# P times V of a sliding-window attention kernel on two 64-row tiles

## The chip, the cores and the metric

The kernel runs on one core of a Trainium2 chip. The metric is device time in microseconds, the time of the whole program. The kernel before took 688.97 us in the median of 3 runs (688.08 to 691.63).

## What is computed

One layer mixes two branches over a sequence of 2048 positions of width 512. Branch A is attention with 32 heads of 16 dimensions, in which a query sees its own key and the 255 before it; branch B is a layer norm and a two-layer MLP with 1792 hidden units. A gate per position adds them.

```python
qkv = (x @ wqkv).reshape(B, S, 3, H, Dh).transpose(2, 0, 3, 1, 4)      # H = 32, Dh = 16, W = 256
scores = einsum("bhqd,bhkd->bhqk", q, k) * Dh ** -0.5
mask = (idx[:, None] - idx[None, :] >= 0) & (idx[:, None] - idx[None, :] < W)
p = softmax(where(mask, scores, -1e9), axis=-1)
o = einsum("bhqk,bhkd->bhqd", p, v)                                     # "P times V"
a = o.transpose(0, 2, 1, 3).reshape(B, S, D) @ wo
b = gelu(layernorm(x) @ w1 + b1) @ w2 + b2
out = g * a + (1 - g) * b                                               # g = sigmoid(sum(x * gate_w))
```

## The kernel before, in words

The program has three stages. The first computes q, k and v and the layer norm's statistics. The second, from about 150 to 487 us, does the attention and the MLP's first layer together; the change lies in it. The third computes the attention's output projection and the MLP's second layer. The program's order within an engine is the order in which the Python code issues it: a manual schedule is set, so nothing is moved afterwards.

The second stage is a string of steps written out by hand, `ORDER` (line 38). Each letter is one step that `run` (line 748) issues:

- **S** is `s_pair` (line 353): scores of 128 queries against up to 384 keys for two of the four heads of a pass, only to find the maximum of each query. TensorE writes a pair of PSUM banks (line 362), and VectorE reads it: `copy_predicated` (line 371) folds the mask's corner in, and `tensor_reduce` (line 372) takes the maximum. For the first two query blocks it is line 368 instead.
- **T** is `st_pair` (line 409): the same scores turned round, 128 keys by up to 384 queries, for two heads (line 418). ScalarE takes the exponential out of PSUM into a tile `pts[p, kb]` (line 420), and GpSimd cuts the window's two edges to zero (line 422). A tile `pts[p, kb]` holds four heads by 384 queries for the 128 keys of block `kb`.
- **P** is `pv` (line 429): for four heads and 256 queries (step `j` of 8) it multiplies the `pts` tiles of up to four key blocks by v. v has 17 columns a head, the last of ones, so that the sum of the weights comes out as well, and 32 are loaded. Two P in a row, where the first has an even `j`, become one of 512 queries (`both`).
- **f** is `fill` (line 719): one step of the MLP's first layer, two matmuls of 64 rows and 512 columns (line 651), 24 such steps to a unit. A unit ends with two copies by ScalarE (`copy`, line 136) and two stores.

P is written out on the array as follows. `a` is one bank; head `h` goes to partitions `32 * h` to `32 * h + 32` and so to its own column tile, `tile_position=(0, 32 * h)`, over all 128 rows. The inner products of one key block are cut out at whole blocks of 128 queries: for a step of 256 queries the pieces are 256, 128, 256 and 128 columns wide (768 for each head), and for 512 queries 256, 128, 384, 384, 256 and 128 (1536). The first step of a pass has the last two of four, or the last four of six. The result is copied by ScalarE into `s` (line 449 or 453, recorded at line 136), or, once the S steps have run out (`last`), by VectorE (line 451). Every 512 queries `s` is stored (line 458 through SyncE, one step later; line 460 through ScalarE's queue at the end).

S, T, P and a unit of f each take a pair of PSUM banks from a ring of four pairs, b0 to b3 (`two`, line 117; `choose`, line 114). `PICK` (line 51) says for each whether the oldest pair is taken or the next. A unit of f keeps its pair over 24 steps, so three are left to S, T and P in the meantime. A pair can be written again when the engine that empties it has done so: VectorE for S, ScalarE for T, P and f.

Of the kernel before, what the change touches and what calls it, by code (L numbers as in the profile page):

```python
# [17 lines left out]
ALU = mybir.AluOpType  # L18
# [14 lines left out]
VW = 17  # L33
# [28 lines left out]
def gated_mix_kernel(ctx, tc: tile.TileContext, xt, x2, wq0, wqk, wv, wo, xa, gw, w1, w2, b1, b2, out):  # L62
    nc = tc.nc
    dve, act, pool, pe, sp = nc.vector, nc.scalar, nc.gpsimd, nc.tensor, nc.sync
# [18 lines left out]
    def get(key, tag, bufs, shape, dt=F32):  # L83
        return left[key].tile(list(shape), dt, name=nm(tag), tag=tag, bufs=bufs)
# [18 lines left out]
    def ps(tag, shape=(128, 512)):  # L103
        key, bufs = banks[tag]
        return left[key].tile(list(shape), F32, name=nm("ps_" + tag), tag=tag, bufs=bufs)
# [3 lines left out]
    def pair(tag):  # L109
        if tag not in pairs:  # L110
            pairs[tag] = ps(tag, (128, 2, 512))
        return pairs[tag]

    def choose():
        return ring.pop(int(picks.pop(0)) if picks else 0)

    def two():
        if not ring:
            return ps("x", (128, 2, 512))
        ring.append(choose())  # L120
        return pair(ring[-1])
# [13 lines left out]
    def copy(dst, src):  # L135
        act.activation(dst, src, AF.Copy)  # L136
# [4 lines left out]
    def after(k, fn):  # L141
        todo.setdefault(step[0] + k, []).append(fn)
# [25 lines left out]
    vs = get("ring", "v", 1, (128, NB, VR))  # L168
# [184 lines left out]
    def s_pair(p, qb, pr):  # L353
        if qb == 0 and pr == 0:
            mxs[p] = small("mx", 2, (128, 2, 2, NB))
        assert qb * 128 < held_cols[p]
        n = min(qb + 1, 3) * 128
        t0 = qb * 128 + 128 - n
        o = two()
        for e in range(2):  # L360
            r, k = ((0, 62), (64, 112))[e]
            pe.matmul(o[:, e, :n], qs[pr][r:k, qb * 128:qb * 128 + 128], ks[pr][r:k, t0:t0 + n],  # L362
                      start=True, stop=True)
        m = mxs[p][:, pr, :, qb]
        if qb < 2:
            for e in range(2):
                sc = small("scr", 2, (128, 256), BF16)
                dve.tensor_tensor_reduce(out=sc[:, :n], in0=o[:, e, :n], in1=wide[:, 256 - n:], scale=1.0, scalar=NEG,
                                         op0=ALU.add, op1=ALU.max, accum_out=m[:, e:e + 1])
        else:  # L370
            dve.copy_predicated(o[:, :, :128], tri, o[:, :, 256:384])  # L371
            dve.tensor_reduce(m, o[:, :, :256], mybir.AxisListType.X, ALU.max)  # L372
        if pr and qb % 4 == 3:
            put_max(p, qb - 3)
# [32 lines left out]
    pts, acc = {}, {}  # L407

    def st_pair(p, kb, pr):
        w = min(NB - kb, 3) * 128  # L410
        assert ("m", p, (kb * 128 + w - 1) // 512) in done
        if pr == 0:
            pts[p, kb] = p_tile()
        pt = pts[p, kb][:, 2 * pr:2 * pr + 2]
        o = two()
        for e in range(2):
            r, k = ((0, 64), (64, 114))[e]
            pe.matmul(o[:, e, :w], ks[pr][r:k, kb * 128:kb * 128 + 128], qs[pr][r:k, kb * 128:kb * 128 + w],  # L418
                      start=True, stop=True)
        act.activation(pt[:, :, :w], o[:, :, :w], AF.Exp, scale=0.25)  # L420
        for a, sgn, b in ((0, 1, 0), (256, -1, -1))[:1 + (w == 384)]:
            pool.affine_select(out=pt[:, :, a:a + 128], in_=pt[:, :, a:a + 128], pattern=[[0, 2], [sgn, 128]],  # L422
                               base=b, channel_multiplier=-sgn, compare_op=ALU.is_ge, fill=0.0)

    def flush():
        while late:
            late.pop(0)()

    def pv(p, j, last, both):
        flush()  # L430
        a = two()[:, 0]
        if both:
            parts = ((-1, 0, 128, 256), (-2, 0, 256, 128), (0, 0, 0, 384), (1, 128, 0, 384), (2, 256, 0, 256),
                     (3, 384, 0, 128))[0 if j else 2:]
        else:
            parts = ((-1, 0, 128, 256), (-2, 0, 256, 128), (0, 0, 0, 256), (1, 128, 0, 128))[0 if j else 2:]
        for n, (d, at, fr, w) in enumerate(parts):
            kb = 2 * j + d
            for h in range(4):
                v = (4 * p + h) * VW  # L440
                pe.matmul(a[32 * h:32 * h + 32, at:at + w], vs[:, kb, v:v + 32], pts[p, kb][:, h, fr:fr + w],  # L441
                          start=n == 0, stop=n == len(parts) - 1, skip_group_check=True, tile_position=(0, 32 * h))
        if j % 2 == 0:
            sums.append(sums.pop(0))
            acc[p] = sums[-1]
        s = acc[p]
        o = j % 2 * 256
        if both:
            copy(s, a)
        elif last:  # L450
            dve.tensor_copy(s[:, o:o + 256], a[:, :256])
        else:
            copy(s[:, o:o + 256], a[:, :256])
        if j % 2 or both:
            j += both
            to = osc[p, :, (j - 1) * 256:(j + 1) * 256]
            if lt:
                after(1, lambda: sp.dma_start(to, s))
            else:
                act.dma_start(to, s)  # L460
# [258 lines left out]
    def fill():  # L719
        if cur[0] is None:  # L720
            assert {("w", jobs[0][0]), ("y", jobs[0][1], KT - 1)} <= done
            cur[0] = mlp1_unit(*jobs.pop(0))
        if next(cur[0], 0) == 0:
            cur[0] = None

    def block(p, kb):
        if kb % 2 == 0:
            if kb and p + 1 < 8:
                load_stacks(p + 1, kb * 128 - 256, 256)
            if not kb and p:  # L730
                load_stacks(p, S - 256, 256)
        tick()
        if p in (0, 2, 4) and kb % 2 == 0:
            double(p // 2 + 1, kb // 4, 1 - kb // 2 % 2)
        if p == 7 and kb == LAG:
            early_w2()
        if p == 7 and kb == 12:
            early.extend(load_h(0, f) for f in range(2))
        if p == 7 and kb == 13:
            early_wo(0, 2)  # L740
# [4 lines left out]
    ls = [(p, qb, pr) for p in range(8) for qb in range(NB) for pr in range(2)][2 * (NB - LAG):]  # L745
    lp = [(p, j) for p in range(8) for j in range(NB // 2)]

    def run(order):
        skip = False
        for a, b in zip(order, order[1:] + " "):  # L750
            if skip:
                skip = False
                continue
            spot[0] += 1
            for n in sorted(n for n in soons if n <= spot[0]):
                for fn in soons.pop(n):
                    fn()
            flush()
            if a == "T":
                p, kb, pr = lt.pop(0)  # L760
                if not pr:
                    block(p, kb)
                st_pair(p, kb, pr)
            elif a == "S":
                s_pair(*ls.pop(0))
            elif a == "P":
                p, j = lp.pop(0)
                skip = b == "P" and j % 2 == 0
                if skip:
                    lp.pop(0)  # L770
                pv(p, j, not ls, skip)
                spot[0] += skip
            else:
                fill()

    run(ORDER + 6 * "f")
    flush()
    for f, (gelu, _) in enumerate(early):
        gelu()
    held = {"b0", "b1", "b2", "b3"} - set(ring)  # L780
    for x in held:
        mate = x[0] + str(int(x[1]) ^ 1)
        ring.remove(mate)
        ring.insert(0, mate)
    run("P")
    ring.insert(0, ring.pop())
    used = {ring[0]} | held
# [184 lines left out]
```

## Time and profile before

| what | value |
|---|---|
| median of the runs | 688.97 us (688.08 to 691.63) |
| the profiled execution's own time | 689.64 us |
| its span, first to last instruction | 687.8 us |
| granted TensorE clock | 0.999 |
| TensorE, VectorE, ScalarE, GpSimd busy | 681.1, 476.4, 384.6, 265.9 us |
| second stage, P: matmul records, steps | 1856 records, 60 steps (4 of them of 512 queries) |
| second stage, P: evacuations | 54 by ScalarE, 6 by VectorE |

All durations in the text come from this one execution, whose own time is 0.67 us above the median. In a row of the groups or of the timeline stand the line, the engine, the operation, what it writes and reads, the shapes and the number of instructions; PE is TensorE's matmuls and PEld its weight loads, DVE is VectorE, ACT ScalarE and POOL GpSimd. A copy through `copy` stands at line 136 whatever it copies. The first number of a timeline row is its start in us from the span's start, the second the time that it covers, and a bracket gives the idle time of the engine before it and what ended that. A full-precision matmul of P stands in the records twice: the code issues 928 and the profile has 1856.

### The profile page before, as it was taken

To read this page: it belongs to the slowest core of one execution; us is meant where nothing else is said; L and a number is where in the kernel's file an instruction comes from. 1 tells how busy PE (TensorE), PEld (TensorE's weight loads), DVE (VectorE), ACT (ScalarE), POOL (GpSimd) and SP (SyncE) were. 2 spreads that over 40 slices of the span, in tenths; PEclk is the share of its full clock that TensorE was granted. 3 is DMA by queue.
4 is the path that set the end of the run, shared out by engine and by line. 5 is a ranking of instruction groups with operands and counts; after the bars stand their busy time and mean duration, and the time that the engine had idled before them with its cause. 6 is when DMAs were issued, how large, how long until landed. Compare 5 with 4: busy or idle time off the path is not lost.

```text
span 687.8 us, 15593 instructions
## 1 busy us (share of the span) xinstructions
PE 681.1 (99%) x5674; PEld 535.5 (78%) x5674; DVE 476.4 (69%) x970; ACT 384.6 (56%) x637; POOL 265.9 (39%) x622
## 2 busy tenths in 40 slices
PE   9999999999999999999999999999999999999997
PEld 6887777877768777877787777777787888888886
DVE  6737789968777787777686877855575545556454
ACT  6438453457677776877758777687633224123231
POOL 6800156426666664765656566568000000000000
PEclk9999999999999999999999999999999999999999
DMA  8998888786575767566676555527876450841801
GB/s 322 354 290 266 278 262 267 217 253 224 176 211 173 247 211 228 174 214 188 190 240 207 168 185 153 178 96 240 288 238 204 143 173 5 275 126 41 253 1 62
DMA packets 89620, 137.91 MB, mean 200 GB/s; under 512 B 13160, under 2 KB 36648, under 8 KB 89416
## 3 DMA queue, kind: packets, MB, share of 16 engines
q1 hardware_dynamic: 81384, 128.72, 59.1%
q10 hardware_dynamic: 8160, 8.19, 3.9%
q8 instruction: 45, 0.74, 0.4%
q14 instruction: 31, 0.25, 0.1%
HBM read 81.53 MB, written 54.30 MB: 197 GB/s over the span
## 4 chain that ended last, share of the span: by engine, by line
PE 96%; ACT 1%; DVE 1%; DMA 1%; issue 0%; POOL 0%; SPq 0%; DVEq 0%; ACTq 0%
PE ps_b L651 22%; PE ps_a L881 22%; PE ps_b L441 13%; PE ps_d L308 12%; PE ps_b L418 7%; PE ps_b L362 7%; PE ps_d L338 7%; PE ps_o L850 6%; PE ps_d L295 1%; PE ps_x L362 1%; DMA qk<-qk 1%; PE ps_x L279 1%; ACT x L420 0%; DVE us L895 0%; DVE us L889 0%; ACT pb L420 0%
## 5 line engine op out<-in xcount | busy, mean ns | idle before, releaser
L651 PE MATMUL ps_b<-x,w 64*128 64x512 f32 x1344 | 207.1, 393 | 0.0
L881 PE MATMUL ps_a<-x,t 128*128 128x512 f32 x648 | 150.2, 389 | 0.2 <-DVE t L711 0.2
L372 DVE TENSOR_REDUCE mx<-ps_b 128x2 f32<-128x512 f32 x208 | 144.1, 693 | 7.1
L881 PEld LDWEIGHTS ps_a<-x,t 128*128 128x128 f32 x648 | 121.5, 188 | 26.2 <-DVE t L711 0.6
L651 PEld LDWEIGHTS ps_b<-x,w 64*128 64x128 f32 x1344 | 127.4, 186 | 10.5 <-ACT x L136 0.3
L371 DVE COPY_PREDICATED ps_b<-tri,ps_b 128x256 f32<-128x256 uint8 x208 | 88.4, 425 | 52.7 <-PE ps_b L362 40.6
L422 POOL TENSOR_SCALAR_AFFINE_SELECT pa<-pa 128x256 f32<-128x256 f32 x192 | 74.2, 414 | 57.7 <-ACT pa L420 56.7
L420 ACT ACTIVATE pa<-ps_b 128x768 f32<-128x768 f32 x96 | 76.5, 813 | 24.7 <-PE ps_b L418 13.3
L418 PE MATMUL ps_b<-qk 50*128 50x384 f32 (+5 forms) x512 | 87.8, 339 | 0.1
L308 PE MATMUL ps_d<-x,w 128*128 128x512 f32 x360 | 84.7, 390 | 0.0
L362 PE MATMUL ps_b<-qk 62*128 62x384 f32 (+3 forms) x472 | 83.0, 345 | 1.0 <-DMA qk<-qk 0.8
L308 PEld LDWEIGHTS ps_d<-x,w 128*128 128x128 f32 x360 | 67.3, 188 | 14.5 <-issue 0.5
L420 ACT ACTIVATE pb<-ps_b 128x768 f32<-128x768 f32 (+2 forms) x96 | 66.2, 706 | 20.5 <-PE ps_b L418 9.7
L422 POOL TENSOR_SCALAR_AFFINE_SELECT pb<-pb 128x256 f32<-128x256 f32 x160 | 62.2, 415 | 37.4 <-ACT pb L420 36.9
L707 ACT ACTIVATE t<-t,b1s 128x512 f32<-128x512 f32 x56 | 38.6, 716 | 44.0 <-DMA t<-hp 43.6
L418 PEld LDWEIGHTS ps_b<-qk 50*128 50x128 f32 (+1 forms) x512 | 48.8, 184 | 16.0 <-issue 3.2
L422 POOL TENSOR_SCALAR_AFFINE_SELECT x<-x 128x256 f32<-128x256 f32 x128 | 49.3, 414 | 29.7 <-ACT x L420 29.3
L420 ACT ACTIVATE x<-ps_b 128x768 f32<-128x768 f32 x64 | 50.7, 813 | 14.0 <-PE ps_b L418 9.7
L362 PEld LDWEIGHTS ps_b<-qk 62*128 62x128 f32 (+1 forms) x472 | 45.1, 184 | 17.2 <-issue 3.9
L338 PE MATMUL ps_d<-wv,x 128*128 128x512 f32 x192 | 46.7, 394 | 0.0
L850 PE MATMUL ps_o<-w,t 128*128 128x512 f32 x192 | 46.1, 389 | 0.0
L441 PE MATMUL ps_b<-pa,v 128*32 128x128 f32 (+2 forms) x704 | 42.9, 345 | 0.3 <-ACT x L420 0.2
(96 smaller groups left out, 757.1 us busy)
## 6 DMA issues: line engine op xcount, KB each, us to landing
qk<-qk SPq DMA_DIRECT2D x112, 196.0 KB
t<-hp SPq DMA_DIRECT2D x56, 256.0 KB
hp<-t SPq DMA_DIRECT2D x54, 256.0 KB
qk<-t SPq DMA_DIRECT2D x48, 256.0 KB
osc<-x SPq DMA_DIRECT2D x31, 256.0 KB
t<-in_w SPq DMA_DIRECT2D x28, 256.0 KB
w<-w SPq DMA_DIRECT2D x28, 256.0 KB
qk<-t ACTq DMA_DIRECT2D x24, 256.0 KB
```

The lines of the kernel that those rows point to most:

```text
L308: pe.matmul(o, a[:, dt * 128:(dt + 1) * 128], b[:, dt * C:(dt + 1) * C], start=n == 0, stop=n == 11)
L338: pe.matmul(o, x[:, a:a + 128], wvs[dt][:, k], start=n == 0, stop=n == 11)
L362: pe.matmul(o[:, e, :n], qs[pr][r:k, qb * 128:qb * 128 + 128], ks[pr][r:k, t0:t0 + n], start=True, stop=True)
L371: dve.copy_predicated(o[:, :, :128], tri, o[:, :, 256:384])
L372: dve.tensor_reduce(m, o[:, :, :256], mybir.AxisListType.X, ALU.max)
L418: pe.matmul(o[:, e, :w], ks[pr][r:k, kb * 128:kb * 128 + 128], qs[pr][r:k, kb * 128:kb * 128 + w], start=True, stop=True)
L420: act.activation(pt[:, :, :w], o[:, :, :w], AF.Exp, scale=0.25)
L422: pool.affine_select(out=pt[:, :, a:a + 128], in_=pt[:, :, a:a + 128], pattern=[[0, 2], [sgn, 128]], base=b, channel_multiplier=-sgn, comp ...
L441: pe.matmul(a[32 * h:32 * h + 32, at:at + w], vs[:, kb, v:v + 32], pts[p, kb][:, h, fr:fr + w], start=n == 0, stop=n == len(parts) - 1, sk ...
L651: pe.matmul(o[:, e], w[kt // 4][r:r + 64, k, m:m + 128], y[r:r + 64, a:a + C], start=n == 0, stop=n == 23)
L850: pe.matmul(a, x[:, g], wos[g][:, k], start=n == 0, stop=n == 11)
L881: pe.matmul(accs[c][b], x[:, b * 128:(b + 1) * 128], w, start=f == 0 and n == 0, stop=f == FT - 1 and n == 2)
```

## The change

`pv` no longer multiplies all 128 keys of a block at once. It takes the upper and the lower 64 keys apart: rows 0 to 63 of the array for the one and rows 64 to 127 for the other (`tile_position=(64 * r, 32 * h)`), with the result of each in a bank of its own of the pair that `two` gives. Each half has its own span of queries: 64 keys reach 320 queries, not 384. The pieces of a half are sorted by width, widest first, and the two lists are issued side by side: four matmuls (one a head) of the upper half, four of the lower, then the next pieces. For 256 queries that makes pieces of 256, 192, 128 and 64 columns in each half. At the end ScalarE copies the first bank into `s`, and VectorE adds the second bank to it. The branch for `last` is gone, so the six steps whose result VectorE copied have ScalarE's copy and VectorE's sum too. `ORDER`, `PICK`, the ring and every other step are as they were.

```diff
-    def pv(p, j, last, both):
+    def pv(p, j, both):
         flush()
-        a = two()[:, 0]
-        if both:
-            parts = ((-1, 0, 128, 256), (-2, 0, 256, 128), (0, 0, 0, 384), (1, 128, 0, 384), (2, 256, 0, 256),
-                     (3, 384, 0, 128))[0 if j else 2:]
-        else:
-            parts = ((-1, 0, 128, 256), (-2, 0, 256, 128), (0, 0, 0, 256), (1, 128, 0, 128))[0 if j else 2:]
-        for n, (d, at, fr, w) in enumerate(parts):
-            kb = 2 * j + d
-            for h in range(4):
-                v = (4 * p + h) * VW
-                pe.matmul(a[32 * h:32 * h + 32, at:at + w], vs[:, kb, v:v + 32], pts[p, kb][:, h, fr:fr + w],
-                          start=n == 0, stop=n == len(parts) - 1, skip_group_check=True, tile_position=(0, 32 * h))
+        a = two()
+        q, w = 256 * j, 512 if both else 256
+        parts = []
+        for r in range(2):
+            seen = []
+            for kb in range(max(2 * j - 2, 0), 2 * j + w // 128):
+                k = kb * 128
+                fr, to = max(q, k + 64 * r * (kb > 0)), min(q + w, k + 64 * r + 320)
+                seen.append((fr - to, kb, fr - q, to - q, fr - k, to - k))
+            parts.append(sorted(seen))
+        for n, pieces in enumerate(zip(*parts)):
+            for r, (_, kb, *at) in enumerate(pieces):
+                rows = slice(64 * r, 64 * r + 64)
+                for h in range(4):
+                    v = (4 * p + h) * VW
+                    pe.matmul(a[32 * h:32 * h + 32, r, at[0]:at[1]], vs[rows, kb, v:v + 32], pts[p, kb][rows, h, at[2]:at[3]],
+                              start=n == 0, stop=n == len(parts[0]) - 1, skip_group_check=True, tile_position=(64 * r, 32 * h))
...
-        if both:
-            copy(s, a)
-        elif last:
-            dve.tensor_copy(s[:, o:o + 256], a[:, :256])
-        else:
-            copy(s[:, o:o + 256], a[:, :256])
+        copy(s[:, o:o + w], a[:, 0, :w])
+        dve.tensor_tensor(out=s[:, o:o + w], in0=a[:, 1, :w], in1=s[:, o:o + w], op=ALU.add)
```

More of the change, by code (lines that the diff above doesn't have):

```diff
@@ L770, in run @@
                     lp.pop(0)
-                pv(p, j, not ls, skip)
+                pv(p, j, skip)
                 spot[0] += skip
```

## The prediction, made before the changed kernel was run

> **What bounds the kernel now.** I read the page's totals and its chain first, then the waits of the second stage, then P's groups by shape, then the timeline around single P steps.
>
> ```profile
> PE 681.1 (99%) x5674; PEld 535.5 (78%) x5674; DVE 476.4 (69%) x970; ACT 384.6 (56%) x637; POOL 265.9 (39%) x622
> PE 96%; ACT 1%; DVE 1%; DMA 1%; issue 0%; POOL 0%; SPq 0%; DVEq 0%; ACTq 0%
> ```
>
> TensorE is busy all the time and carries 96% of the chain. So TensorE's columns are what the change can save, and TensorE's waiting is what it can cost. The waits of the second stage (150 to 490 us), matmuls first, weight loads below, say how much waiting there is:
>
> ```profile
> PE ps_b L362 <- DMA qk<-qk: 0.8, 1, 0.8
> PE ps_b L441 <- ACT x L420: 0.2, 1, 0.2
> PEld ps_b L441 <- ACT x L136: 5.6, 23, 0.3
> ```
>
> The matmuls waited 1.0 us in 340. The weight loads waited more, and the third row tells where: in 23 of the 60 P steps the load stood until ScalarE's copy of a P (line 136 into x) had ended, 0.24 us each. That is the copy of the P before: the next one takes the same PSUM pair. It shows only at the loads, because TensorE has just come out of other matmuls; but nothing is left over there. The timeline shows one such place whole:
>
> ```profile
> 165.01 0.16 PEld L441 LDWEIGHTS ps_b<-pa,v 128*32 128x32 f32 x8 [0.25 <-ACT x L136]
> 165.01 0.64 PE L441 MATMUL ps_b<-pa,v 128*32 128x256 f32 x8
> ...
> 165.69 0.62 PE L441 MATMUL ps_b<-pb,v 128*32 128x256 f32 x8
> ...
> 166.12 0.40 PE L441 MATMUL ps_b<-x,v 128*32 128x128 f32 x8
> 166.45 0.30 PEld L362 LDWEIGHTS ps_b<-qk 62*128 62x128 f32 x4 [0.20 <-ACT pb L420]
> 166.45 0.61 PE L362 MATMUL ps_b<-qk 62*128 62x384 f32 x4
> 166.59 0.39 ACT L136 ACTIVATE x<-ps_b 128x256 f32<-128x256 f32 x1 [0.30 <-PE ps_b L441]
> ...
> 166.90 0.34 PE L418 MATMUL ps_b<-qk 64*128 64x384 f32 x2
> 167.00 0.43 DVE L371 COPY_PREDICATED ps_b<-tri,ps_b 128x256 f32<-128x256 uint8 x1 [0.90 <-ACT x L136]
> 167.17 0.16 PEld L441 LDWEIGHTS ps_b<-x,v 128*32 128x32 f32 x8 [0.25 <-ACT x L136]
> ```
>
> A P runs from 165.01 to 166.45, 1.44 us. Two S and a T follow, 0.72 us. ScalarE copies P's result from 166.59 to 166.98. At 167.17, 0.19 us after the copy, the next P starts on the same pair. So the pair is wanted again 0.72 us after P's matmuls, and the copy takes 0.53 of these.
>
> **TensorE's columns.** P's matmul groups by shape:
>
> ```profile
> L441 PE MATMUL ps_b<-pa,v 128*32 128x256 f32 x320 | 25.3, 388 | 0.3 <-ACT x L420 0.2
> L441 PE MATMUL ps_b<-pb,v 128*32 128x256 f32 x320 | 24.8, 381 | 0.0
> L441 PE MATMUL ps_b<-x,v 128*32 128x256 f32 x256 | 20.1, 385 | 0.0
> L441 PE MATMUL ps_b<-pa,v 128*32 128x128 f32 x320 | 16.4, 273 | 0.0
> L441 PE MATMUL ps_b<-pb,v 128*32 128x128 f32 x320 | 16.1, 273 | 0.0
> L441 PE MATMUL ps_b<-x,v 128*32 128x128 f32 x256 | 13.1, 273 | 0.0
> L441 PE MATMUL ps_b<-pa,v 128*32 128x384 f32 x64 | 6.0, 490 | 0.0
> ```
>
> These are 896 records of 256 columns, 896 of 128 and 64 of 384. Four heads run side by side and every matmul is recorded twice, so divided by 8 they make 46,080 columns, each passed twice. The price is in the timeline: the eight records that start at 165.69 (four heads of 256 columns, twice) give way to the next at 166.12, so 512 columns take 0.43 us, 0.84 ns a column. P's streaming is 46,080 x 2 x 0.84 ns = 77.4 us. The mean durations in the rows are no price; records overlap.
>
> After the change the two halves lie on different rows and in different banks, and I let them run together: a step costs the wider piece of each pair. That is 640 columns for 51 of the steps (256, 192, 128 and 64 in place of 768), still 384 for the five first steps of 256 queries, 1088 in place of 1152 for three first steps of 512, and 1280 in place of 1536 for one. The sum is 39,104, that is 6,976 fewer, and 6,976 x 2 x 0.84 ns = **11.7 us saved**, 0.22 us on a usual P. That halves run together is shown by the MLP steps, which set two matmuls of 64 rows beside each other (the pairs of 64x512 below), and four column tiles beside each other by P itself; eight tiles at once no row shows.
>
> The narrowest piece, 64 columns, must cost its 0.054 us and not more. The nearest rows are a T of 128 columns and what follows it:
>
> ```profile
> 312.24 0.23 PE L418 MATMUL ps_b<-qk 64*128 64x128 f32 x2
> 312.30 0.45 PE L651 MATMUL ps_b<-x,w 64*128 64x512 f32 x2
> ```
>
> The next pair starts 0.06 us behind it and runs 0.06 longer than the 0.39 of its group: a load of 128 weights a row takes about 0.12 us of the array, so I estimate a quarter, 0.03, for 32, which fits under 0.054. From the other side, a piece of 128 columns now takes 0.11 us; if that were a floor, 52 pieces, twice each, would give back 52 x 2 x 0.054 = 5.6 us. I take nothing, and keep 5.6 for the range.
>
> The eight records that start at 165.69 show no sum of starts: four tiles take exactly the 0.84 ns a column that the streaming asks. [...]
>
> **The second bank.** Every P gets a VectorE sum out of PSUM, behind ScalarE's copy:
>
> ```profile
> L451 DVE COPY x<-ps_b 128x256 f32<-128x256 f32 x6 | 2.6, 426 | 12.1 <-PE ps_b L441 7.0 <-DMA hp<-t 5.1
> L889 DVE TENSOR_TENSOR us<-ps_a,b2s 128x512 f32<-128x512 f32 x4 | 2.5, 682 | 0.0
> L133 DVE TENSOR_TENSOR w<-wv,w 128x128 fp32r<-128x128 f32 x8 | 2.1, 289 | 0.6 <-ACT w L136 0.4
> ```
>
> A sum over 512 columns takes 0.68 us, one over 128 takes 0.29, so over 256 0.42; the copy of 256 takes 0.43. Work for VectorE: 56 x 0.42 + 4 x 0.68 less the six copies of 0.43 = 23.7 us, over a stage in which it has this load:
>
> ```profile
> 250.00:300.00 50.00, 50.00 (x646) 38.67 (x644) 38.23 (x86) 37.34 (x58) 31.05 (x83) 1.00 0.64 201
> ```
>
> 38.2 us of 50 (third pair), 76%; with 23.7 more in 340 it is 83%. VectorE does not become the bound by its sum. What counts is when the pair is free: the sum waits for the copy, so it comes 0.42 + 0.05 (a handover) later. In the place above: 167.45 in place of 166.98, measured against the same end of P. P's being shorter doesn't help, since the 0.72 us between P's end and the next use hold only S and T. The next P starts 0.05 after the release, and has 0.19 now, so it comes 0.33 us late, and TensorE stands, since matmuls start in order. The other kind of place has an S, a T or an MLP unit on the pair next, not a P:
>
> ```profile
> 309.34 0.44 PE L418 MATMUL ps_b<-qk 64*128 64x384 f32 x2
> 309.54 0.38 ACT L136 ACTIVATE x<-ps_b 128x256 f32<-128x256 f32 x1 [0.63 <-PE ps_b L441]
> 309.62 0.63 PE L651 MATMUL ps_b<-x,w 64*128 64x512 f32 x4
> 309.97 0.18 PEld L418 LDWEIGHTS ps_b<-qk 64*128 64x128 f32 x2 [0.16 <-ACT x L136]
> 310.09 0.34 PE L418 MATMUL ps_b<-qk 64*128 64x384 f32 x2
> ```
>
> The copy ends at 309.92, the load starts at 309.97 and the matmul at 310.09, when the MLP pairs before it are through: a delay of 0.47 costs 0.45 here. Other places have more room. I take 0.33 us for each of the 54 steps that ScalarE empties now: **17.8 us**; bounds are none (the room is always found) and 54 x 0.47 = 25. The six last steps lose 0.39 (the copy ahead of the sum) where VectorE has few other tasks, about 1 us in all.
>
> Behind the sum, on VectorE, stand the S steps that TensorE issues right after P: at 167.00 above a `copy_predicated` starts that would wait until about 167.45. Their pairs come free as much later, but are wanted only after the user that already came 0.33 late; the rest is about 0.1 us a P where there is no room, at a third of the steps 2 us; bounds 0 and 5. The stores of `s` leave 0.5 us later through SyncE's queue, and the last one through ScalarE's; who reads them does so in the next stage, so nothing.
>
> **Sum.** -11.7 + 17.8 + 1 + 2 = +9 us, on the execution's 689.64, and as much on the median of 688.97: **698 us**.
>
> [...]
>
> **Rivals.**
>
> *The sum is hidden (faster).* If the next user of P's pair could start 0.47 us later without TensorE noticing, the 11.7 would remain, less some 2: 680 us. It decides at the room behind the copy: 0.05 to 0.2 us in the two places above, so it needs over twice that. For it: not every place is alike, and each wait lets ScalarE and VectorE catch up. Against it: 23 loads ended on this very copy.
>
> *The halves do not run together.* If the second half can only start when the first half's second pass does, each step gets a piece's length behind at every change of width, and 256+256+256+192+192+128+128+64+64 = 1536 passed columns are what 2 x 768 were. Nothing is saved, and the stalls stay: 709 us. If they ran one after the other it would be 77,312 columns, 52 us more than now, near 760. For it: eight tiles are not in the trace. Against: each of the two kinds of tiling is.
>
> *The way in and out gets cheaper.* Between 64-row and 128-row tiles there is a gap: the loads of 165.01 and 166.45 stood idle 0.25 and 0.20 us, of which about 0.1 at each end is no streaming. With 64 rows throughout, it may go. The gap behind P is part of the 0.72 us that cover the copy, so only the one ahead counts, 0.1 x 53 = 5 us: 693, no change. [...]
>
> **How the numbers follow.** The smallest change that a measurement of this kernel can tell is about 0.5%, 3.4 us: 685.5 to 692.4 is "same". The forecast (stalls outweigh columns) has 0.60, and alone reaches from 692 to 706. The hidden sum has 0.17, some of it ending just within "same". Halves apart have 0.11, all slower. The cheaper switch has 0.12, half of it within "same". Faster 0.16, same 0.14, slower 0.70. The range that holds it 8 times in 10 cuts off half the hidden cases and the serial ones: 684 to 712.
>
> **What would show it.** In the changed profile: P's records twice as many, 3712, a usual P 1.2 us long; in the waits of the weight loads VectorE's sum in the place of line 136, with matmuls now waiting 15 to 20 us on it in all; VectorE near 500 us busy. If P takes 1.4 us the halves do not overlap; if P takes 1.2 us and the matmuls hardly wait, the forecast is wrong by its stalls and the time is near 680.

## The result, and the profile after

The changed kernel takes **712.02 us** in the median of 4 runs (710.84 to 712.67) against 689.26 for the kernel before beside it (4 runs, 688.08 to 691.63): 1.0322 times as long, 95% interval 1.0302 to 1.0342. It is slower, as forecast, but by 22.8 us and not by 9, and lies 0.02 us beyond the range's upper end of 712. The profiled execution took 712.67 us at a granted clock of 0.999. The page's totals, its queue of instruction packets and its chain after the change:

```profile
PE 683.9 (96%) x7530; PEld 547.1 (77%) x7530; DVE 492.9 (69%) x1024; ACT 386.5 (54%) x643; POOL 268.7 (38%) x622
...
q8 instruction: 59, 0.97, 0.6%
...
PE 66%; DMA 10%; DVE 9%; ACT 7%; issue 3%; SPq 3%; POOL 2%; ACTq 0%; DVEq 0%
```

TensorE is busy 96% of the span where it was 99%, and other engines have come into the chain. The changed P has 7530 - 5674 = 1856 records more, hence 3712, as forecast. The second line belongs to the argument further down, where q8's packets are set against TensorE's instructions; before it read

```profile
q8 instruction: 45, 0.74, 0.4%
```

The waits of the second stage (150 to 515 us; the columns are us in total, times, longest) now say where TensorE stands:

```profile
PEld ps_b L446 <- issue: 16.6, 28, 1.5
PEld ps_b L418 <- DVE x L454: 8.6, 18, 0.7
PE ps_b L446 <- DVE x L454: 7.7, 19, 0.6
PEld ps_b L362 <- DVE x L454: 6.1, 10, 1.5
...
PE ps_b L362 <- DVE x L454: 2.6, 6, 1.3
...
PE ps_b L446 <- issue: 2.4, 3, 1.3
...
PE ps_b L418 <- DVE x L454: 2.3, 9, 0.4
```

Line 454 is VectorE's sum. Matmuls wait 7.7 + 2.6 + 2.3 = 12.6 us on it, where all matmul waits of the stage were 1.0 us before; the prediction's sign was 15 to 20. The first row, P's weight loads with "issue" as their releaser, is for the most part the same wait under another name, as e12 shows below. The timeline shows one place whole:

```profile
166.76 0.61 PE L446 MATMUL ps_b<-pa,v 64*32 64x128 f32 x32
...
167.30 0.44 PE L418 MATMUL ps_b<-qk 64*128 64x384 f32 x2
...
167.50 0.38 ACT L136 ACTIVATE x<-ps_b 128x256 f32<-128x256 f32 x1
...
167.76 0.34 PE L418 MATMUL ps_b<-qk 64*128 64x384 f32 x2
...
167.91 0.42 DVE L454 TENSOR_TENSOR x<-ps_b,x 128x256 f32<-128x256 f32 x1 [0.90 <-ACT x L136]
168.25 0.42 DVE L371 COPY_PREDICATED ps_b<-tri,ps_b 128x256 f32<-128x256 uint8 x1
...
168.48 0.42 PE L446 MATMUL ps_b<-pb,v 64*32 64x256 f32 x4 [0.38 <-DVE x L454]
```

P gave way to the T at 167.30; the copy runs to 167.88, the sum to 168.33, and the next P, on the same pair, starts at 168.48: TensorE stood for 0.38 us. The group of these sums, and the stretch of the stage that the prediction read (busy us of PE, PEld, DVE, ACT, POOL; granted clock; DMA share; GB/s):

```profile
L454 DVE TENSOR_TENSOR x<-ps_b,x 128x256 f32<-128x256 f32 x56 | 23.8, 425 | 39.9 <-ACT x L136 39.7
```

```profile
250.00:300.00 50.00, 47.50 (x840) 38.20 (x840) 41.40 (x104) 34.85 (x54) 28.42 (x76) 1.00 0.64 197
```

A sum takes the 0.42 us of the forecast. VectorE sat idle 39.9 us ahead of these sums, nearly all of it until ScalarE's copy ended, and in the trace each of the 60 sums starts 0.03 us behind the end of its copy: VectorE's other work held none of them back. TensorE misses 2.5 us of 50 where it missed none, and VectorE, at 83%, is not the bound.

To see all such places I matched the steps of the two traces one to one (the order of the steps is the same) and took, for each, how much later it starts against the step before it. The 23.0 us between the two profiled executions are:

| part | forecast, us | trace, us |
|---|---|---|
| P itself, first matmul to the next step, without fetch stalls | -11.7 | -7.2 |
| the next user of a P's pair (23 P, 21 T, 11 S, 2 f, and with 0.20 us the stage's last P, whose pair was a T's) | +17.8 and +1 | +18.65 |
| all other steps of the stage | +2 | +3.3 |
| stalls for instructions, mostly within P | not counted | +4.6 |
| ahead of the stage and behind it | 0 | +2.6 and +1.1 |

I don't put the last row down to the change: ahead of the stage the kernels of this study that differ only behind that point lie between 0.5 us below and 2.7 above the kernel before, and behind the stage, where they don't differ, between 0.7 below and 3.5 above.

### The profile page after: what moved, and what is told of

It reads as the page before. It is cut to its first block, busy times and chain, and to the rows that moved or that the text cites. A ratio compares the mean times of both kernels' runs of the same rounds, so it can differ in the third digit from the quotient of the medians.

```text
span 710.9 us, 19436 instructions
## 1 busy us (share of the span) xinstructions
PE 683.9 (96%) x7530; PEld 547.1 (77%) x7530; DVE 492.9 (69%) x1024; ACT 386.5 (54%) x643; POOL 268.7 (38%) x622
## 4 chain that ended last, share of the span: by engine, by line
PE 66%; DMA 10%; DVE 9%; ACT 7%; issue 3%; SPq 3%; POOL 2%; ACTq 0%; DVEq 0%
PE ps_b L652 18%; PE ps_a L882 15%; PE ps_b L446 8%; PE ps_o L851 6%; PE ps_b L418 5%; PE ps_d L308 5%; PE ps_b L362 5%; PE ps_d L338 3%; DVE x L454 2%; ACT x L136 2%; DMA qk<-qk 2%; DVE mx L372 2%; DMA t<-in_w 2%; ACT t L136 2%; DMA t<-hp 1%
## 5 line engine op out<-in xcount | busy, mean ns | idle before, releaser
L418 PE MATMUL ps_b<-qk 64*128 64x384 f32 (+5 forms) x512 | 89.9, 347 | 2.8 <-DVE x L454 2.3
L454 DVE TENSOR_TENSOR x<-ps_b,x 128x256 f32<-128x256 f32 (+1 forms) x60 | 26.6, 443 | 46.8 <-ACT x L136 46.6
L446 PE MATMUL ps_b<-pb,v 64*32 64x64 f32 (+3 forms) x1280 | 48.3, 299 | 7.3 <-DVE x L454 6.1
L446 PE MATMUL ps_b<-pa,v 64*32 64x192 f32 (+5 forms) x1408 | 52.3, 315 | 1.1 <-DVE x L454 0.4
```

The source lines that it names most:

```text
L446: pe.matmul(a[32 * h:32 * h + 32, r, at[0]:at[1]], vs[rows, kb, v:v + 32], pts[p, kb][rows, h, at[2]:at[3]], start=n == 0, stop=n == len(p ...
L454: dve.tensor_tensor(out=s[:, o:o + w], in0=a[:, 1, :w], in1=s[:, o:o + w], op=ALU.add)
```

## The experiments

Each ran beside the kernel before on the same chip; kernels of different rows compare by their ratios. The columns behind the ratio are from the traces: by how much a usual P is longer than before (median), by how much a P comes late that takes the pair of the P just ahead (median of 24, with the stage's last P), the sum over all next users of a P's pair, and the stalls for instructions over 0.4 us, counted as told under the first experiment.

| run | median, us | ratio, 95% interval | usual P | P behind P late | next users | fetches |
|---|---|---|---|---|---|---|
| the change | 712.02 | 1.0322 (1.0302 to 1.0342) | -0.147 | 0.459 | 18.65 | 4.6 |
| e1_no_sum | 691.78 | 1.0046 (1.0028 to 1.0063) | -0.142 | 0.007 | 1.17 | 5.5 |
| e2_sum_only | 705.95 | 1.0246 (1.0230 to 1.0261) | 0.000 | 0.306 | 13.99 | 0 |
| e3_uncut | 713.35 | 1.0350 (1.0330 to 1.0371) | +0.076 | 0.292 | 13.41 | 0.6 |
| e4_narrow_first | 707.09 | 1.0253 (1.0224 to 1.0282) | -0.137 | 0.323 | 15.96 | 0.4 |
| e8_split_copy | 713.37 | 1.0353 (1.0332 to 1.0373) | -0.147 | 0.461 | 18.72 | 4.3 |
| e9_one_copy | 702.05 | 1.0179 (1.0164 to 1.0195) | -0.147 | 0.219 | 9.86 | 5.7 |
| e10_one_copy_narrow | 696.60 | 1.0101 (1.0075 to 1.0126) | -0.138 | 0.092 | 6.62 | 1.8 |
| e11_no_sum_narrow | 689.10 | 0.9992 (0.9970 to 1.0013) | -0.138 | 0.002 | 0.64 | 4.8 |
| e12_lower_first | 703.90 | 1.0214 (1.0196 to 1.0232) | -0.138 | 0.344 | 16.04 | 0.7 |

The theory to test: TensorE's shorter P is real but small, and the time is set by when a P's pair comes free. Its rivals: VectorE's added load, the eight tiles, the pace of the exponents whatever P does.

### One half of the change at a time

```diff
 # e1_no_sum, against the changed kernel
-        dve.tensor_tensor(out=s[:, o:o + w], in0=a[:, 1, :w], in1=s[:, o:o + w], op=ALU.add)
 # e2_sum_only, against the kernel before (for all three branches of the copy)
+        w = 512 if both else 256
+        copy(s[:, o:o + w], a[:, :w])
+        dve.tensor_tensor(out=s[:, o:o + w], in0=a[:, :w], in1=s[:, o:o + w], op=ALU.add)
```

> Leaves out VectorE's sum, so the keys of the lower halves are missing from the result; the matmuls, the order and ScalarE's copy are those of the changed kernel. Theory A (the changed kernel loses where the next user of P's pair waits for the sum, 18.7 us by the trace, and a P is shorter by 0.147 us only): about 712 - 19 - 2 = 691, between 686 and 693, with a P of 1.29 us from its first matmul to the next load. Rival B (the matmuls would have given the whole 11.7 us, and something else in the changed kernel hides it): 677 to 682. Rival C (the waits at P's pair are a by-product, the time is lost by the array's changes of mode and by eight tiles at once): 705 or more.

> The kernel before with its 128-row matmuls, and VectorE adds the same bank once more after ScalarE's copy (numerators and denominators are both doubled, so the quotient stays). Theory A: the sum alone costs what the changed kernel's waits came to, 18.7 us, and some 2 to 4 us behind it: 708 to 712. Theory as predicted, 0.33 us for a P: 17.8 + 1 + 2 = 710. Rival C: the loss came with the matmuls, so this is within 3 us of the kernel before, 687 to 692.

The sum alone costs 705.95 - 689.30 = 16.7 us; 13.99 of them stand in the trace at the pair's next users, a P behind a P 0.306 us late where the prediction had 0.33. The trace names the sum, line 450 there:

```profile
PEld ps_b L441 <- DVE x L450: 13.2, 23, 0.7
...
PE ps_b L441 <- DVE x L450: 6.0, 23, 0.4
```

Nothing else was touched, so this part of the change needs no eight tiles. The matmuls alone (e1), which should have gained, lose 2.5 us. P is 0.142 us shorter in the median and no pair is late, and the waits of the stage name one thing:

```profile
PE ps_b L446 <- issue: 4.7, 4, 1.7
```

"Issue" is time in which nothing that the profile shows held the engine. The longest such stall of the changed kernel lies in the middle of a P:

```profile
420.57 0.52 PEld L446 LDWEIGHTS ps_b<-x,v 64*32 64x32 f32 x20
420.62 0.35 PE L446 MATMUL ps_b<-pb,v 64*32 64x192 f32 x4
420.73 0.49 PE L446 MATMUL ps_b<-x,v 64*32 64x128 f32 x19
...
422.56 0.34 PE L446 MATMUL ps_b<-x,v 64*32 64x64 f32 x13 [1.34 <-issue]
```

The DMA queues between 419.5 and 422 us, where q8 had a single packet in 2.5 us, at 420.0:

```profile
q1 hardware_dynamic: 134, 0.15, 19.0%
q8 instruction: 1, 0.02, 3.0%
```

By the page's name for q8 that packet is code. 0.97 MB in 59 packets are 16.4 KB each; over TensorE's 15,244 instructions in the trace (7530 loads, 7530 matmuls, 184 others) that makes 258 to a packet, and in the kernel before, with 45 packets of 16.4 KB for 11,480 instructions (two times 5674, 132 others), 255. From these two I estimate a block, as I call it from here on, at 256 instructions. So I numbered TensorE's instructions in the order of their starts, from the first in the trace, and divided the number of the first one behind each stall by 256. In the changed kernel the stalls that end at 239.6, 382.7 and 422.6 us leave the remainders 192, 192 and 193; the four of e1 leave 192 to 194, and four of e8, four of e9 and three of e11 leave 192 or 193. In all of them the last q8 packet had ended 1.2 to 1.6 us before. Stalls for other reasons leave any remainder (104, 76, 66, 221, 242 in the changed kernel). The reading that fits is that TensorE had run through its code faster than it came; the matmuls stood for 0.55 to 1.73 us. The kernel before, with 1856 loads and 1856 matmuls fewer, shows no such stall.

### What a P costs by itself

```diff
 # e3_uncut: the spans of before, 768 columns, still on eight tiles and two banks
-                fr, to = max(q, k + 64 * r * (kb > 0)), min(q + w, k + 64 * r + 320)
+                fr, to = max(q, k), min(q + w, k + 384)
 # e4_narrow_first
-            parts.append(sorted(seen))
+            parts.append(sorted(seen, reverse=True))
```

> The changed kernel with the halves' spans not cut to 320 queries: 768 columns a step in place of 640, pieces of 256, 256, 128 and 128, still eight tiles and two banks. If columns are the only price: 6,976 x 2 x 0.84 ns = 11.7 us more, 724, and a P of 1.51 us. Theory A (narrow pieces of 64 columns cost more than their columns, the others cost theirs): P comes back to the 1.44 us of before, 0.147 x 54 = 8 us more, 720. If eight tiles cost by their number, whatever their width: a P stays near 1.29 us and the time near 712.

> The changed kernel with each half's pieces sorted the other way, the 64-column ones first and the 256-column ones last. Theory A1 (instructions come to the array at some 17 ns for a load and its matmul, so eight narrow ones in a row run the queue dry; ahead of P the queue is full): P falls from 1.29 to about 1.22 us, and the time to about 708, less what earlier need of the newest tile takes. Theory A2 (a piece of 64 columns has a floor of about 0.09 us a pass wherever it stands): P stays at 1.28 to 1.30 us and the time within 2 us of 712.

e3's timeline of TensorE has a usual P from 165.01 to 166.52, where the kernel before took 165.01 to 166.45 for the same columns:

```profile
165.01 0.66 PE L446 MATMUL ps_b<-pa,v 64*32 64x256 f32 x16
165.46 0.64 PE L446 MATMUL ps_b<-x,v 64*32 64x256 f32 x16
165.90 0.70 PE L446 MATMUL ps_b<-pa,v 64*32 64x128 f32 x32
166.52 0.44 PE L418 MATMUL ps_b<-qk 64*128 64x384 f32 x2
```

So the two halves do run together (one after the other would be twice that), but eight tiles in two banks, with twice the instructions, cost 0.076 us a P more than four in one; which of the three it is, e3 doesn't tell. The columns are worth what was counted: from e3 to the change P falls from 1.514 to 1.290 us, 0.224, against 0.22 forecast.

e3's time, 713.35 us, missed the 720 and 724 of its expectation, though its 51 usual P are 11.4 us longer in all than the changed kernel's: the next users lose 5.2 us less and the fetches cost 4.0 less. A P's first load reads an older exponent tile there, and the row of P's loads with "issue" is 2.8 us, where the changed kernel has 16.6. e12 does that alone.

In e4 the 64-column pieces are in front and P still gains only 0.137, so it is not the narrow piece at the end that costs. The 0.076 us of e3 stand against the nothing that I took.

e4 also took 4.9 us off the changed kernel. A P behind a P is late by 0.323 us in place of 0.459, and fetches cost 0.4 us in place of 4.6. Why the first, e12 tells. The order has a price of its own: it needs the newest exponent tile at once, and between 482 and 497 us TensorE's matmuls stand four times, 2.0 us in all, until GpSimd has cut a tile's edges.

### Covering the late pair with other work

```diff
 # 88 f steps moved directly behind P steps; one place of many, before and after
-"...SffTfSfffSTPTSTPSSTPSffTSffff..."
+"...SffTfSfSTPffTSTPffSSTPSffTSff..."
```

> The changed kernel with its matmuls, copies and sums as they are; only the written-out order differs: 88 of its f steps (pairs of the MLP, 0.39 us each) move from longer runs nearby to directly behind a P, so that two of them lie between most P and the next user of its pair. The theory (TensorE stands because the pair is freed later; 18.65 us of the 22.8 are at the pair's next user) expects that these stalls go for the most part, since 0.78 us of other matmuls now cover the 0.46 that came late: 18.65 to about 3, so 694 to 697 us; the 4 to 5 us of stalls within single P steps stay. The rival (VectorE's load as a whole, or P's eight tiles, make the time) expects no change from it: 708 to 714. A second rival (the f steps are needed where they stood, and their absence opens waits of S and T steps on ScalarE and VectorE there) expects 700 to 710, with the new waits on ScalarE's exponentials; the kernel before in the same order would then be slower as well.

> As the run e5, with the pieces of a P issued narrow first. That order took 5 us off the changed kernel in e4, by a shorter wait at the first load (one semaphore in place of two) and by fewer stalls within single P steps. The theory expects that with the pair's wait covered only the second of these is left to gain, 3 to 4 us on e5: 690 to 694 us, the kernel before within 1%. The rival (load of VectorE) expects e4's 707 again.

> The kernel before with the same rewritten order as e5: the control. The theory expects no change beyond what 88 moved steps do by themselves, since nearly nothing waited behind a P there: 689 within 3 us, perhaps 1 to 2 us less where its 0.24 us waits of the weight loads go. If the order opens waits elsewhere, it is 693 or more, and as much is to be taken off e5 and e6.

All three missed. e5 took 738.00 us (ratio 1.0720, 1.0695 to 1.0746), e6 735.79 (1.0678, 1.0661 to 1.0695), and the control e7, the kernel before in the new order, 731.76 (1.0621, 1.0602 to 1.0641). The second rival named in e5 held, and by far more than its price: an f step taken away from where it stood opens a wait there. The control's waits in the stage:

```profile
PEld ps_b L418 <- DVE mx L372: 10.6, 38, 0.8
PEld ps_b L441 <- ACT t L136: 9.6, 10, 1.1
...
PE ps_b L441 <- ACT t L136: 6.5, 10, 0.8
PEld ps_b L441 <- ACT pa L420: 6.0, 13, 1.0
```

P waits for ScalarE's copy of an MLP unit and for the exponents, T for VectorE's maxima, and of matmul waits there were 1.0 us in all before. What can be read with care is the difference under one order: with these other waits in the same places the change costs 6.2 us (738.00 to 731.76) and not 22.8. That fits a late pair that hides behind another wait, but the orders differ too much to prove it.

### Freeing the pair sooner

```diff
 # e8_split_copy, for j > 0
+            low = pts[p, 2 * j - 2][:, :w // 256, :256]
...
+            dve.tensor_copy(low, a[:, 1, :w].rearrange("p (x n) -> p x n", n=256))
+            pool.tensor_tensor(out=whole, in0=low, in1=whole, op=ALU.add)
 # e9_one_copy, for j > 0 and 256 queries
+            halves = pts[p, 2 * j - 2][:, :2, :256]
+            copy(halves, a[:, :, :256])
+            pool.tensor_tensor(out=s[:, o:o + w], in0=halves[:, 1], in1=halves[:, 0], op=ALU.add)
```

> The changed kernel, in its own order, with the pair freed by two engines at once: ScalarE copies the first bank as before, VectorE copies the second into a tile of exponentials that nobody reads any more, and GpSimd adds the two in SBUF (the first step of each group of heads keeps the sum). VectorE's work is the same, GpSimd gets 48 sums more. The theory (the pair is held by a copy and then a sum, one behind the other) expects the pair 0.4 us sooner: of the 18.65 us at its next users 3 to 6 stay (VectorE is not always free at P's end), so 695 to 700 us. The rival (VectorE's load, whatever its order) expects 708 to 714; GpSimd's added work may show in its own exponent tiles and would give back 1 to 3 us.

> The changed kernel with both banks of a usual P copied out by one ScalarE instruction (512 columns, 0.60 us by the four such rows) into a tile of exponentials that nobody reads any more, and the two halves added by GpSimd in SBUF; 48 steps of 60, the others as they were. The pair is then free 0.13 + 0.60 us after P's end in place of 0.13 + 0.385 + 0.03 + 0.425, 0.24 us sooner. The theory (the pair's release sets TensorE's stall) expects the median lateness of a P behind a P to fall from 0.46 to about 0.22, and the 18.65 us at next users to about 8 to 10, so 701 to 704 us. The rival (after e5 and e8: what costs is VectorE's or the exponents' chain, not the pair) expects no change, 710 to 714.

> As e9, with the pieces of a P issued narrow first. e4 against the changed kernel gave 5 us by that alone. The theory expects both gains together, 5 and 9 us: 695 to 699 us, still behind the kernel before; a P behind a P late by about 0.1 us. If instruction fetches fall within P steps again, up to 4 us more.

e8 missed, because its edit did not do what it was for. VectorE's copy as one place of the timeline has it, and what its line waited for:

```profile
168.21 0.39 ACT L136 ACTIVATE x<-ps_b 128x256 f32<-128x256 f32 x1 [0.68 <-PE ps_b L446]
...
168.62 0.42 DVE L457 COPY x<-ps_b 128x256 f32<-128x256 f32 x1 [0.99 <-ACT x L136]
```

```profile
its engine sat idle before it (us, times) until:
  ACT x L136: 40.5, 42
```

It starts 0.02 us behind ScalarE's copy, not beside it: ahead of these copies VectorE sat idle 42 times, 40.5 us in all, until a copy by ScalarE had ended, though the two read different banks of the pair. The pair came free when it did before, and lateness and time stayed (0.461 us, 713.37). The run tells nothing between theory and rival.

e9 does. One instruction of ScalarE takes both banks out in 0.60 us, and the next P starts 0.15 us behind it:

```profile
167.80 0.45 PE L418 MATMUL ps_b<-qk 64*128 64x384 f32 x2
...
168.04 0.60 ACT L136 ACTIVATE pa<-ps_b 128x512 f32<-128x512 f32 x1
...
168.78 0.74 POOL L456 TENSOR_TENSOR x<-pa 128x256 f32<-128x256 f32 x1
168.79 0.42 PE L446 MATMUL ps_b<-pb,v 64*32 64x256 f32 x4 [0.19 <-ACT pa L136]
```

The pair is free 0.24 us sooner, a P behind a P comes 0.219 us late in place of 0.459, and the time falls by 10 us to 702.05, both as the theory had it. VectorE lost 51 sums here and GpSimd got them (the page counts 673 GpSimd instructions, 622 in the changed kernel), so e9 by itself does not part the earlier release from a lighter VectorE. The changed kernel's trace does: no sum there waited for VectorE's other work, only for the copy. Sums on GpSimd alone gain nothing (e8, 52 of them). e2 shows the other side: a sum added to untouched matmuls makes a P behind a P 0.306 us late. e10 adds the two gains, 696.60 as expected, still 1% behind. A good part of what is left stands at one P, from 470.7 us on, after which the next step comes 3.3 us late (0.8 in e4, 1.4 in e9). Its matmuls wait for GpSimd, which has a sum ahead of the exponent tile's edges now, while the order narrow first needs that tile at once:

```profile
PE ps_b L446 <- POOL pa L422: 2.1, 3, 1.0
```

### The matmuls without the sum, once more

> e1 (the changed matmuls without VectorE's sum; the keys of the lower halves are left out of the result) with the pieces narrow first. e1 took 692 us in place of the 678 that the columns alone gave. The theory blames the instruction fetches within P steps (about 4 us), a second semaphore wait ahead of P's first weight load (about 2), and a chance stall before the second stage (1 to 2): with narrow first the first two go, and the 7 to 8 us that P is shorter by appear: 681 to 685 us. The rival (P's shorter time is taken back by the engines that TensorE then waits for, whatever the order) expects 689 to 692.

The theory missed: 689.10 us, level with the kernel before, is where the rival had it. The trace keeps the theory's reading of the parts, though: P is 0.138 us shorter in the median, some 7 us in all; no pair is late; and from the stage's start to its last P it takes 2.9 us less, not 7, for the most part because fetches cost 4.8 us, once between an S and a T:

```profile
439.32 0.44 PE L362 MATMUL ps_b<-qk 62*128 62x384 f32 x2
...
441.08 0.39 PE L418 MATMUL ps_b<-qk 64*128 64x256 f32 x2 [1.32 <-issue]
```

Ten runs spread from 685.07 to 692.27. What failed is the thought that the order narrow first avoids the fetches. It moves where in P the blocks end, but e4 gives TensorE the same instructions (15,191 in its trace, 15,190 here) and loses 0.4 us by fetches, so the place alone does not decide. In e4 TensorE stands for the pairs in between (15.96 us in all), which leaves the code more time to come; that would explain it, but no run tests it.

### Which weight load stands first

```diff
-            for r, (_, kb, *at) in enumerate(pieces):
+            for r, (_, kb, *at) in reversed(list(enumerate(pieces))):
```

> The changed kernel with one edit: of each pair of pieces the lower half's is issued first. The first weight load of a usual P then reads an older tile of exponentials and waits for the pair alone, not for GpSimd's masked tile as well. The theory (the second semaphore wait adds about 0.09 us between the pair's release and P's first matmul, in 24 P behind a P and about as much in some of the others) expects 2 to 4 us less than the changed kernel: 708 to 710; release to matmul 0.055 in place of 0.147. If the instruction fetches fall elsewhere than within P steps, up to 4 us less again. The rival (that 0.09 is the time of reading 64-row loads, or of another thing) expects 711 to 713 and 0.147 still.

The edit swaps neighbours and took 8 us, more than expected. TensorE's semaphore instructions ahead of P's loads, in the changed kernel and then in e12 (count, ns, first and last start):

```profile
L446 PEldq EVENT_SEMAPHORE  x60: 51/51/51, 155.8 to 504.0; - x60
```

```profile
L446 PEldq EVENT_SEMAPHORE  x10: 51/51/51, 155.0 to 474.5; - x10
```

Widest first, upper half first, a P's first load reads the newest but one of the exponent tiles and needs GpSimd's mark beside the pair: two waits, and I take the 50 further semaphore instructions, 51 ns each, for the second of them. With the lower half first the tile is an older one, and the pair's is the only wait. The row of P's loads with "issue", 16.6 us in the changed kernel, is 1.0 us here, and the same wait stands under VectorE's sum:

```profile
PEld ps_b L446 <- DVE x L454: 13.2, 23, 0.8
```

From the sum's end to the next P's first matmul it is 0.055 us in place of 0.147:

```profile
167.11 0.43 DVE L454 TENSOR_TENSOR x<-ps_b,x 128x256 f32<-128x256 f32 x1 [0.80 <-ACT x L136]
...
167.59 0.13 PEld L446 LDWEIGHTS ps_b<-pa,v 64*32 64x32 f32 x5 [0.59 <-DVE x L454]
167.59 0.42 PE L446 MATMUL ps_b<-pa,v 64*32 64x256 f32 x4 [0.27 <-DVE x L454]
```

The next users fall by 2.6 us, the 2 to 4 of the theory, and fetches by 3.9, which the expectation had as a possibility: 50 semaphore instructions less shift the blocks by up to 50 places against the P steps. That the shift is the cause is not shown.

### The change only where there is room

```diff
 # e13_far_only, against the kernel before; NEAR: the 24 P steps with a P next on their pair
+        cut = j > 0 and not both and not last and (p, j) not in NEAR
...
+        if cut:
+            halves = pts[p, 2 * j - 2][:, :2, :256]
+            copy(halves, a[:, :, :256])
+            pool.tensor_tensor(out=s[:, o:o + w], in0=halves[:, 1], in1=halves[:, 0], op=ALU.add)
```

> The kernel before, with the two row tiles of 64 keys only in the P steps whose pair is next taken by a T, an S or an MLP unit, not by another P, and which have all four key tiles (about 28 of 60), narrow pieces first, both banks copied by one ScalarE instruction and added by GpSimd; the other P steps as before. The theory (the columns save 0.14 us a P; a pair that is freed later costs where a P follows on it; extra instructions cost fetches) expects 28 x 0.14 = 3.9 us saved, 1 to 2 us of late pairs and about 1 us of fetches left: 686 to 689 us, level with the kernel before or just ahead. The rival (cutting costs wherever it is done, since the exponents' chain sets the pace) expects 692 or more, in proportion to e10's loss of 7 us: 28 of 60 is 3.

687.70 us in the median of 12 runs (685.77 to 691.70) against 689.93 beside it: ratio 0.9974, 0.9955 to 0.9994. The records show that 23 steps were cut, not 28 (6410 - 5674 = 736 records, 32 a step), so the columns are worth 3.2 us. The matmuls' waits of the stage are four in all:

```profile
PE ps_b L452 <- issue: 1.4, 1, 1.4
PE ps_b L422 <- DMA qk<-md: 0.6, 1, 0.6
PE ps_b L679 <- ACT pb L140: 0.2, 1, 0.2
PE ps_b L366 <- DMA qk<-qk: 0.2, 1, 0.2
```

One fetch, at the 193rd instruction of a block, and nothing on a P's pair. This is the only version that comes out below the kernel before, by less than the 0.5% that the prediction called a change. The rival, that a cut costs wherever it is made, had 692 or more and falls.

## Why the prediction was right and wrong

**Right: the sign, and the largest term.** The stalls at the pair's next user were forecast at 18.8 us and are 18.65. The reason was right too: e2 has the cost with the old matmuls, e9 has it nearly halved where the pair is free 0.24 us sooner, and VectorE's load did not make the pairs late, since each sum started 0.03 us behind the end of its copy. The weight loads wait for VectorE's sum, and VectorE was busy 492.9 us (forecast: near 500). Without the sum (e1) the matmuls gain nothing, where the prediction had 11.7 us.

**Right in sum, not in its parts.** A P behind a P is 0.459 us late, not 0.33, and T and S users are less late (medians 0.173 and 0.237). The sum alone is 0.306 (e2). The rest has two parts. P's last matmul is shorter now but ScalarE's copy does not come sooner by as much: it starts 0.344 us behind the start of P's last matmul, 64 columns wide, and 0.340 in e2, where that is 128 wide. Against the end of P's last record, which the profile models, that is 0.128 and 0.067. And the second wait ahead of the first load adds 0.09 (e12). The statement "P's being shorter doesn't help" was right for another reason as well.

**Wrong: the step "TensorE's columns".** It had 11.7 us saved, 0.22 on a usual P, and nothing for eight tiles in place of four. The columns are worth 0.224 us, but eight tiles in two banks cost 0.076 a P (e3), so that 0.147 are left, 7.2 us in all. The row that it rested on, four tiles at 0.84 ns a column, did not carry over to eight.

**Wrong: a term that was missing.** 1856 more loads and as many more matmuls came with 14 blocks of code more (45 packets, then 59). In a P's last pieces 32 matmuls start within 0.54 us (166.76 to 167.30 above), 17 ns each, and now and then, by the reading above, a block comes late: 4.6 us in the profiled run, of which no step of the prediction spoke, though the page of before had q8's line. Columns and fetches together, 4.5 + 4.6, are most of the 14 us between forecast and result; 1.3 more lie in the other steps of the stage (3.3 us, of which e2, with the sum alone, has 2.3), within the bound of 5 that was kept for them; 3.7 lie outside the stage and show no tie to the change.

**The rivals.** The sum is not hidden: 18.65 us. The halves do run together: P is 1.29 us long, and e3's 1.51 carries the columns of before. The way in got no cheaper: in e11, with neither a late pair nor the second wait, a P behind a P starts 0.002 us later than before and not 0.1 sooner, and where the pair is late the second wait makes it dearer. None of them had the fetches.

## What to carry to other kernels

When matmuls are cut into more and smaller ones, price three things beside the columns: the release of the accumulator as the next user on its bank sees it (all engines that empty it, one behind the other), the instructions themselves (their count, their blocks, an added wait ahead of the first load), and the further tiles of a group. Of the three ways tried here, the second accumulator bank was cheapest to empty by one instruction of one engine, with the sum done later on a copy (e9, 702.05 us against 712.02 and e8's 713.37); and of the versions with the whole result only the one that cuts at steps whose bank nobody wants soon came out below the kernel before (e13, 687.70 us against 689.93). A run of independent steps that looks like spare cover may be cover already (e7, the moved order alone, 731.76 against 688.87): try a moved order on the kernel before first.

## What the runs showed of the hardware that was not expected

- TensorE stood 0.55 to 1.73 us at a time where, by the count of e1, a block of instructions came late: at the 192nd to 194th instruction of 256 in the changed kernel, e1, e8, e9, e11 and e13. Where in the code that place is, and why only some blocks are late, no run tells; nearly as many instructions (15,191 and 15,190) lost 0.4 us in e4 and 4.8 in e11.
- Eight 64x32 tiles in two banks cost 0.076 us a P more than four 128x32 tiles in one over the same columns (e3). Narrow first, a P was 0.137 us shorter than before, widest first 0.147 (e4 and the changed kernel), so the order of the pieces did not win the 0.076 back; its cause stays open.
- The changed kernel has a semaphore instruction of 51 ns ahead of 60 of P's loads, e12 ahead of 10; from the pair's release to the next P's first matmul it is 0.147 us there and 0.055 in e12.
- The copy that empties P starts 0.340 us behind the start of P's last matmul where that has 128 columns (e2) and 0.344 where it has 64 (the changed kernel): here a group that ended on a shorter matmul was not emptied sooner by its whole saving.
